# Sparse attention ahead of two feed-forward layers: transposes as two 64-query row tiles, ninth blocks two units at a time, the scale in the minimum pass, input loads spread out

## The chip, the cores and the metric

The kernel runs on one core of a Trainium2 chip. The metric is device time in microseconds (us) of one execution; the median of the runs is compared. TensorE is called PE here, VectorE DVE, ScalarE ACT, GpSimd POOL; SP is the engine whose queue issues most of the DMAs.

## The reference

```python
def _attn_ref(q, k, v, tau):                      # each (4, 8, 576, 64)
    scores = np.matmul(q, k.transpose(0, 1, 3, 2)) / np.sqrt(q.shape[-1])
    thresh = np.max(scores, axis=-1, keepdims=True) - tau
    scores = np.where(scores >= thresh, scores, -1e9)
    attn = np.exp(scores - np.max(scores, axis=-1, keepdims=True))
    attn = attn / (np.sum(attn, axis=-1, keepdims=True) + 1e-09)
    return np.matmul(attn, v)

x = _attn_ref(q, k, v, tau)                       # -> (2304 tokens, 512)
h = x @ w_in;  x = (h * np.tanh(softplus(h))) @ w_out     # 512 -> 2048 -> 512
y = ((x @ w_a) * (x @ w_b)) @ w_out2                      # 512 -> 1536 -> 512
```

The weights of the two feed-forward layers come in as 64-bit floats; the kernel makes 32-bit ones of them.

## The kernel before

Attention runs over 16 pairs of heads (`pairs`), and a pair over five **units** `c` = 0 to 4. Units 0 to 3 are *full*: 128 queries of both heads, so two score rows of 576 keys in each partition. Unit 4 is *half*: the last 64 queries of both heads, stacked on the 128 partitions. There are 80 units, and `attention()` walks them in a software pipeline. In iteration `n` (85 of them) the engines work on different units:

- PE transposes the masked weights of unit n-2 (`turned`), multiplies the transposed weights of unit n-4 with V (`weighted`), and makes the scores of unit n+1 (`scores`);
- DVE takes the minimum of the negated scores of unit n, a head at a time, and copies them out of PSUM in the same pass (`least`), then masks unit n-1 and sums its rows (`mask`); behind the masks of a half unit stands the reciprocal of the sums (`invert`);
- POOL adds tau to the minimum (`bars`, tile `te`), which the mask of the next iteration reads;
- ACT takes the exponential of unit n (`expo`) and copies the transposed blocks from PSUM to SBUF (`pt`, and `pth` for a half unit).

Every engine works in program order. The whole stage is written inside `tc.manual_schedule()`: nothing reorders it.

A full unit's masked weights `pm` are 9 blocks of 128 columns: 576 keys of one head, then 576 of the other. Before, each block is one 128x128 transpose with the identity; blocks 0 to 3, 4 to 7 and 8 fill three buffers of `ps_t`, and the ninth is issued behind the next scores. A half unit has 4 blocks and one of 64 columns. The score matmuls of a full unit work in two row tiles: head 0 on partitions 0 to 63, head 1 on 64 to 127, each into a bank of its own (`sp`, one pair of buffers in all, since a full unit takes both). `weighted` uses two column tiles of 64, and the half unit's scores and the transposes use the whole array.

`scale_q` is an ACT pass over the queries with the factor `nsc` (minus 1/8, or zero for a negative tau), a pair ahead. `convert` walks the 15 weight blocks that are narrowed from 64 to 32 bits inside attention (`narrow`: two passes on ACT, a shift on DVE, an integer addition on POOL, a sign on ACT, a product, then a DMA to DRAM); a block is asked for every fifth unit, so there is one in each pair. Row sums go through `send_inverse` (a transpose, a copy, three small DMAs to `rd`) and come back as a broadcast `inv` (`load_inverse`); `send` multiplies and stores the pair's result to `xd`. From unit 50 on the inputs of the first feed-forward layer are read back (`prepare`) and split in high and low parts between the units, and so is its first weight block.

The feed-forward layers are `pipeline()`: gaps of PE products with ACT and DVE work planned into each. The last results leave through `leave`, from three buffers `ys`.

Of the kernel before, what the change touches and what calls it, by code (L numbers as in the profile page):

```python
# [43 lines left out]
def tile_attn_mish_bilinear(ctx, tc, qd, kd, vd, vd2, tau, w_in, w_out, w_a, w_b, w_out2, out):  # L44
# [427 lines left out]
    def leave(st, ps, c, kind):  # L472

        if kind == "c":
            ys[c] = ys_p.tile([128, 2 * NH], F32, tag="ys", name=f"ys{st.i}_{c}", bufs=3)
        y = ys[c]
        end = st.layer and st.s == NS - 1
        dst = y[:, 0:512] if kind == "c" else y[:, 512:768]
        if end and c % 2:
            V.tensor_copy(dst, ps)  # L480
        else:
            A.activation(dst, ps, AF.Copy)  # L482
        cols = slice(0, 512) if kind == "c" else slice(512, 768)
        if st.layer:
            t0 = 2 * st.s * NH
            (nc.scalar if end and c % 2 else nc.sync).dma_start(
                out=out[c * 128:(c + 1) * 128, t0 + cols.start:t0 + cols.stop], in_=dst
            )
        elif kind != "c":
            nc.scalar.dma_start(out=y1d[st.s][:, c], in_=y)  # L490
# [113 lines left out]
    with late_pools:  # L604
        at = late_pools.enter_context(tc.tile_pool(name="at", bufs=1, side="right"))
        ps_t = late_pools.enter_context(tc.tile_pool(name="ps_t", bufs=3, space=PSUM, side="right"))
# [8 lines left out]
        def load_qk(pi):  # L615
# [4 lines left out]
            qs = qk.tile([128, 640], F32, tag="qs", name=f"qs{pi}", bufs=2)  # L620
# [5 lines left out]
            return dict(q=q, k=k, qs=qs)  # L626

        def scale_q(d, cols):
            A.activation(d["qs"][:, cols], d["q"][:, cols], AF.Copy, scale=nsc)
# [11 lines left out]
        def warm(n):  # L641

            warmed.append(n)
            w = ps_t.tile([128, 4, 128], F32, tag="tp", name=f"warm{len(warmed)}")
# [3 lines left out]
        ph = at.tile([128, 5, 128], F32, name="ph")  # L648
        pth = at.tile([128, 5, 128], F32, name="pth")
# [19 lines left out]
        def scores(u, d):  # L669
# [4 lines left out]
            for half in range(2):  # L674
                keys = slice(half * 288, half * 288 + 288)
                for h, sp in enumerate(u["sp"]):
                    if u["h"] == 2:
                        r, cols = HEADS[h], slice(u["c"] * 128, u["c"] * 128 + 128)
                        PE.matmul(sp[:, half, 0:288], d["qs"][r, cols], d["k"][r, keys], start=True, stop=True)  # L679
                    else:  # L680
                        PE.matmul(sp[:, half, 0:288], d["qs"][:, 512:640], d["k"][:, keys], start=True, stop=True)  # L681

        def least(u, h):

            if h == 0:
# [3 lines left out]
                scalar1=1.0, scalar2=None, op0=ALU.mult, op1=ALU.min, accum_out=u["m"][:, h:h + 1],  # L689
# [29 lines left out]
        def send_inverse(pi):  # L719

            b, p = pairs[pi]
            tp = ps_t.tile([128, 4, 128], F32, tag="tp", name=f"tr{pi}")
            PE.transpose(tp[0:9, 0], pair[pi]["r"], ident)
            rt = at.tile([9, 128], F32, tag="rt", name=f"rt{pi}", bufs=2)
            A.activation(rt, tp[0:9, 0], AF.Copy)
            for h in range(2):
                nc.sync.dma_start(
                    out=rd[p][b][h:h + 1, 0:512].rearrange("o (c n) -> (o c) n", n=128), in_=rt[4 * h:4 * h + 4]
                )
            nc.sync.dma_start(  # L730
                out=rd[p][b][:, 512:576], in_=rt[8:9].rearrange("o (h n) -> o h n", h=2)
            )

        def turned(u, j0, m):

            pm, pt = u["pm"], u["pt"]
            tp = ps_t.tile([128, 4, 128], F32, tag="tp", name=f"tp{u['nm']}_{j0}")
            if u["h"] == 1 and j0 == 4:
                PE.transpose(tp[0:64, 0], pm[:, 4, 0:64], ident)
                return lambda: A.activation(pt[0:64, 4], tp[0:64, 0], AF.Copy)  # L740
# [73 lines left out]
        def attention():  # L814
# [3 lines left out]
            scale_q(data[0], slice(0, 128))  # L818
            warm(6)
            scale_q(data[0], slice(128, 640))  # L820
# [6 lines left out]
            for n in range(len(units) + 5):  # L827
                u, prev, mid = us.get(n), us.get(n - 1), us.pop(n - 2, None)
                old = units[n - 4] if 4 <= n < len(units) + 4 else None
                convert(n, 1)  # L830
                if u:
# [17 lines left out]
                if backs[1:]:  # L849
                    backs[1]()  # L850
# [6 lines left out]
                last = turned(mid, *parts[-1]) if mid else None  # L857
# [4 lines left out]
                if u and c == 3 and pi + 1 < len(pairs):  # L862
                    scale_q(data[pi + 1], slice(0, 640))
                ask(n)
                convert(n, 5)
# [23 lines left out]
                if last:  # L889
                    last()  # L890
                    if mid["c"] == 4:
                        send_inverse(mid["pi"])
# [75 lines left out]
```

## Time and profile before

| | |
|---|---|
| median of 3 runs | 1093.05 us (1092.75 to 1094.0) |
| the profiled execution's own time | 1093.93 us |
| its span, first to last instruction | 1092.1 us |
| PE busy | 1083.9 us, 99% |
| PE weight loads busy | 942.6 us, 86% |
| DVE busy | 813.2 us, 74% |
| ACT busy | 646.8 us, 59% |
| POOL busy | 68.7 us, 6% |
| one pair of heads, 135.70 to 152.54 us | 16.84 us: PE 16.84, DVE 15.11, ACT 15.30, POOL 4.35 |

Attention takes about the first 285 us, the two feed-forward layers the rest. A busy PE is no proof of a PE at its peak, since the ends of matmuls are modelled; starts are recorded, and the distance from one start to the next is what a matmul costs when nothing waits.

### The profile page before, as it was taken

The page shows a single profiled execution, that of the slowest core. Times are in us where ns is not written, and L with a number is a line of the kernel's source. Part 1 is how long each engine was busy: PE and PEld are TensorE (multiplying, and loading weights), DVE is VectorE, ACT ScalarE, POOL GpSimd, SP SyncE. Part 2 cuts the span into 40 slices and gives each one's busy share as a digit, 9 for nine tenths or more (in the row PEclk, how much of TensorE's full clock was granted, in tenths as well). Part 3 has the DMA queues.
Part 4 walks back from the last instruction along what each step waited for, and adds up shares of the span by engine and source line. Part 5 has one row for each costly group of instructions (what it writes and reads, how often), then busy time and mean ns, then how long its engine had stood idle before and what let it go on. Part 6 is the DMA issues. An engine that isn't in the chain of part 4 may idle for free.

```text
span 1092.1 us, 18655 instructions
## 1 busy us (share of the span) xinstructions
PE 1083.9 (99%) x6842; PEld 942.6 (86%) x6842; DVE 813.2 (74%) x1768; ACT 646.8 (59%) x1285; POOL 68.7 (6%) x101
## 2 busy tenths in 40 slices
PE   9999999999999999999999999999999999999998
PEld 7666666666899999999999999999999999999997
DVE  6889889999567787888667897777766657656653
ACT  6999899999656567566565575434343333433321
POOL 2222222222000000000000000000000000000000
PEclk9999999999999999999999999999999999999999
DMA  5456466645669749695498975436314452143401
GB/s 194 132 181 193 144 200 188 200 142 175 197 214 304 256 153 341 252 349 198 164 356 294 318 275 173 156 128 226 129 59 152 159 189 90 49 154 123 170 8 58
DMA packets 77707, 203.14 MB, mean 186 GB/s; under 512 B 6832, under 2 KB 36272, under 8 KB 73776
## 3 DMA queue, kind: packets, MB, share of 16 engines
q1 hardware_dynamic: 73152, 172.29, 47.4%
q10 hardware_dynamic: 4464, 29.66, 6.8%
q8 instruction: 54, 0.88, 0.4%
q14 instruction: 37, 0.30, 0.1%
HBM read 146.01 MB, written 55.91 MB: 185 GB/s over the span
## 4 chain that ended last, share of the span: by engine, by line
PE 97%; ACT 1%; DVE 1%; issue 0%; DMA 0%; ACTq 0%; POOL 0%; POOLq 0%; DVEq 0%
PE acc L462 32%; PE sums_o L761 7%; PE tp L742 7%; PE sp L679 7%; PE sp L681 1%; PE sums_o L765 1%; PE h0i L342 1%; PE warm L646 1%; PE h6i L342 1%; PE h3i L342 1%; PE h7i L342 1%; PE h5i L342 1%; PE h4i L342 1%; PE h2i L342 1%; PE h1i L342 1%; PE h15i L361 1%
## 5 line engine op out<-in xcount | busy, mean ns | idle before, releaser
L462 PE MATMUL acc<-g,woo 128*128 128x256 f32 (+1 forms) x1152 | 225.3, 338 | 0.0
L462 PEld LDWEIGHTS acc<-g,woo 128*128 128x128 f32 x1152 | 181.2, 188 | 16.7
L462 PE MATMUL acc<-g,wop 128*128 128x512 f32 (+1 forms) x864 | 170.7, 338 | 0.0
L462 PEld LDWEIGHTS acc<-g,wop 128*128 128x128 f32 x864 | 137.4, 188 | 13.4 <-DVE g L391 0.8
L687 DVE TENSOR_SCALAR_CACHE_REDUCE s<-sp 128x576 f32<-128x576 f32 x144 | 103.8, 755 | 28.5 <-PE sp L679 24.8
L699 ACT ACTIVATE ex<-s,m 128x576 f32<-128x576 f32 x144 | 109.9, 776 | 5.5 <-DVE s L687 5.5
L743 ACT ACTIVATE pt<-tp 128x512 f32<-128x512 f32 (+1 forms) x192 | 92.4, 494 | 15.3 <-PE tp L742 12.2
L706 DVE SCALAR_TENSOR_TENSOR pm<-s,te,ex 128x576 f32<-128x576 f32 x128 | 99.5, 815 | 0.0
L742 PEld LDWEIGHTS tp<-ident,pm 128*128 128x128 f32 x576 | 64.0, 141 | 23.8 <-ACT ex L699 11.1
L761 PE MATMUL sums_o<-pt,v 128*64 128x256 f32 x640 | 83.2, 389 | 0.3 <-ACT u L771 0.3
L385 DVE TENSOR_TENSOR g<-hs,g 128x384 fp32r<-128x384 f32 x96 | 51.8, 554 | 40.1 <-ACT g L384 32.3
L742 PE MATMUL tp<-ident,pm 128*128 128x128 f32 x576 | 80.2, 278 | 0.6 <-ACT pt L743 0.2
L679 PE MATMUL sp<-k,qs 64*128 64x288 f32 x512 | 80.4, 429 | 0.0
L679 PEld LDWEIGHTS sp<-k,qs 64*128 64x128 f32 x512 | 45.0, 186 | 29.9 <-issue 15.6
L761 PEld LDWEIGHTS sums_o<-pt,v 128*64 128x64 f32 x640 | 40.2, 136 | 25.1 <-issue 5.9
L694 POOL TENSOR_TENSOR te<-m,bar 128x2 f32<-128x2 f32 (+1 forms) x80 | 48.8, 610 | 175.5 <-DVE s L687 175.3
L482 ACT ACTIVATE ys<-acc 128x512 f32<-128x512 f32 (+1 forms) x44 | 21.3, 488 | 30.9 <-PE acc L462 25.4
L390 ACT ACTIVATE g<-s 128x384 fp32r<-128x384 f32 x18 | 9.5, 525 | 39.9 <-DVE s L441 39.6
L390 ACT ACTIVATE g<-c22b 128x384 fp32r<-128x384 f32 x18 | 9.5, 527 | 37.3 <-DVE c22b L441 37.3
L178 DVE TENSOR_TENSOR woo<-wfo,woo 128x512 fp32r<-128x512 f32 x46 | 30.5, 684 | 0.0
L177 ACT ACTIVATE woo<-wfo 128x512 fp32r<-128x512 f32 x46 | 26.7, 627 | 3.0 <-PE acc L462 2.6
L416 DVE TENSOR_TENSOR c22a<-u3a,p5a 128x384 f32<-128x384 f32 x18 | 10.0, 556 | 21.1 <-ACT p5a L414 21.0
(638 smaller groups left out, 2148.1 us busy)
## 6 DMA issues: line engine op xcount, KB each, us to landing
wia<-wpa SPq DMA_DIRECT2D x10, 1792.0 KB
wpi<-wii ACTq DMA_DIRECT2D x7, 1792.0 KB
wii<-wpi SPq DMA_DIRECT2D x7, 1792.0 KB
wfo<-wfo SPq DMA_DIRECT2D x23, 512.0 KB
wpa<-wia ACTq DMA_DIRECT2D x6, 1792.0 KB
v<-vd SPq DMA_DIRECT2D x16, 576.0 KB
rawi<-w_in SPq DMA_DIRECT2D x16, 512.0 KB
rawo<-w_out SPq DMA_DIRECT2D x16, 512.0 KB
```

Source lines behind the costliest of these rows:

```text
L178: lambda: V.tensor_tensor(out=dst()[1], in0=src(), in1=f32(dst()[0]), op=ALU.subtract),
L342: PE.matmul(st.bank, w[:, a, 2 * i + j, c * 128:(c + 1) * 128], x[:, b, c], start=j == c == m == 0, stop=j == c == 1 and m == 2,)
L385: at_gap(gap + 1, lambda: V.tensor_tensor(out=gl, in0=hs, in1=f32(gh), op=ALU.subtract))
L462: PE.matmul(ps, w[:, a, f, c * 128:(c + 1) * 128], st.g[f][:, b, cols], start=st.first and f == 0 and m == 0 and (kind == "c" or c % 2 == ...
L679: PE.matmul(sp[:, half, 0:288], d["qs"][r, cols], d["k"][r, keys], start=True, stop=True)
L687: V.tensor_scalar(out=u["s"][:, h].rearrange("p (a c) -> p a c", a=2), in0=u["sp"][h][:, :, 0:288], scalar1=1.0, scalar2=None, op0=ALU.mul ...
L694: G.tensor_tensor(out=u["te"][:, :n], in0=u["m"][:, :n], in1=bar2[:, :n], op=ALU.add)
L699: A.activation(u["e"][:, h], u["s"][:, h], AF.Exp, bias=u["m"][:, h:h + 1], scale=-1.0)
L706: V.scalar_tensor_tensor(out=u["pm"].rearrange("p a c -> p (a c)")[:, h * S:(h + 1) * S], in0=u["s"][:, h], scalar=u["te"][:, h:h + 1], in ...
L742: PE.transpose(tp[:, i], pm[:, j0 + i], ident)
L743: return lambda: A.activation(pt[:, j0:j0 + m], tp[:, :m], AF.Copy)
L761: PE.matmul(po[r], v[0][:, j + 4 * h, r], pair[pi][c & ~1][:, :, j + 4 * h], start=j == 0, stop=j == 4)
```

## The change

1. **Transposes.** Blocks 0 to 7 of a full unit become two transposes each, of 64 queries (partitions 0 to 63, then 64 to 127) by 128 keys, into two buffers of their own (`tp0`, `tp1`). A half unit has five blocks of this kind; the missing 64 columns of its last one are set to zero once. Each buffer leaves in one ACT copy.
2. **Ninth blocks.** Those of units 0 and 1, and of 2 and 3, are transposed together as whole 128x128 blocks behind the transposes of the later unit, into a third buffer (`tc`), and leave in one copy. The transpose of the inverse sums goes into the same buffer.
3. **Scale.** `scale_q` is gone; `nsc` is the scalar operand of the minimum pass, a value per partition where there was the constant 1.0.
4. **Narrowing.** The product moves from DVE to POOL, and from five units behind the due time to three, where it stands ahead of that unit's `te`.
5. **Order.** `load_inverse` and `send` come two iterations later. The four input loads come at units 49, 54, 59 and 64, their splits from 52 to 70, the first weight block from 66 to 78.
6. **End.** The last wide result of the program gets a buffer of its own.

```diff
@@ narrow @@
-        V.tensor_tensor(out=o, in0=a.bitcast(F32), in1=o, op=ALU.mult)
+        (G if early else V).tensor_tensor(out=o, in0=a.bitcast(F32), in1=o, op=ALU.mult)
@@ leave @@
+            if end and c == 3:
+                ys[c] = raw.tile([128, 2, NH], F32, tag="b00", name=f"ys{st.i}_{c}", bufs=1).rearrange("p i n -> p (i n)")
+            else:
+                ys[c] = ys_p.tile([128, 2 * NH], F32, tag="ys", name=f"ys{st.i}_{c}", bufs=3)
@@ load_qk, scores, least @@
-        def scale_q(d, cols):
-            A.activation(d["qs"][:, cols], d["q"][:, cols], AF.Copy, scale=nsc)
...
-                        PE.matmul(sp[:, half, 0:288], d["qs"][r, cols], d["k"][r, keys], start=True, stop=True)
+                        PE.matmul(sp[:, half, 0:288], d["q"][r, cols], d["k"][r, keys], start=True, stop=True)
...
-                scalar1=1.0, scalar2=None, op0=ALU.mult, op1=ALU.min, accum_out=u["m"][:, h:h + 1],
+                scalar1=nsc, scalar2=None, op0=ALU.mult, op1=ALU.min, accum_out=u["m"][:, h:h + 1],
@@ turned @@
-        def turned(u, j0, m):
...
-            for i in range(m):
-                PE.transpose(tp[:, i], pm[:, j0 + i], ident)
-            return lambda: A.activation(pt[:, j0:j0 + m], tp[:, :m], AF.Copy)
+        def turned(u):
+
+            n = 8 if u["h"] == 2 else 5
+            tiles = [ps_t.tile([128, 8, 64], F32, tag=f"tp{h}", name=f"tp{u['nm']}_{h}") for h in range(2)]
+            for j in range(n):
+                for h, r in enumerate(HEADS):
+                    PE.transpose(tiles[h][:, j], u["pm"][r, j], ident[r, r])
+            moves = [lambda h=h: A.activation(u["pt"][:, 0:n, HEADS[h]], tiles[h][:, 0:n], AF.Copy) for h in range(2)]
+            if u["c"] in (1, 3):
+                t = u["turn"] = ps_t.tile([128, 4, 128], F32, tag="tc", name=f"tc{u['nm']}")
+                both = u["pair"][u["c"] - 1]
+                for i, pm in enumerate((u["pair"]["pm"], u["pm"])):
+                    PE.transpose(t[:, i], pm[:, 8], ident)
+                moves.append(lambda: A.activation(both[:, :, 8], t[:, 0:2], AF.Copy))
+            u["pair"]["pm"] = u["pm"]
+            return moves
@@ attention @@
                 convert(n, 1)
+                convert(n, 3)
...
-                    parts = ((0, 4), (4, 4), (8, 1)) if mid["h"] == 2 else ((0, 4), (4, 1))
-                    backs = [turned(mid, j, m) for j, m in parts[:-1]]
+                    backs = turned(mid)
...
-                last = turned(mid, *parts[-1]) if mid else None
...
-                convert(n, 5)
...
-                if 3 <= n < len(units) + 3 and units[n - 3][1] == 4:
-                    load_inverse(units[n - 3][0])
-                if 8 <= n < len(units) and units[n - 8][1] == 4:
-                    send(units[n - 8][0])
+                if n in range(9, len(units), 5) or n == len(units) + 2:
+                    load_inverse((n - 9) // 5 + (n > len(units)))
+                if 10 <= n < len(units) and units[n - 10][1] == 4:
+                    send(units[n - 10][0])
...
-                if n == 50:
+                if n == 48:
                     loads, rest = prepare(0, 0)
-                    for load in loads:
-                        load()
-                    plan(55, [(2 * k, item) for k, item in rest])
+                    plan(0, zip((49, 59, 64, 54), loads))
+                    plan(0, zip((52, 55, 57, 60, 62, 65, 67, 70), (item for _, item in rest)))
+                if n == 66:
                     load, rest = first_weights(0)
                     load()
-                    plan(56, [(2 * k, item) for k, item in enumerate(rest)])
+                    plan(0, zip((71, 72, 74, 73, 78), rest))
```

On PE, this is what stood in the second pair between the scores of its unit 0 and of its unit 1, where unit 3 of the first pair is transposed (`tp_3`); a matmul of 32-bit floats in such a list is two instructions in the trace, a transpose is one:

```order
L742 MATMUL tp_2_8_388<-ident,pm_2_270 128x128
L742 MATMUL tp_3_0_410<-ident,pm_3_306 128x128 x4
L742 MATMUL tp_3_4_415<-ident,pm_3_306 128x128 x4
L761 MATMUL sums_o<-pt_0_227,v_220 64x256 x4
L679 MATMUL sp_1_0_431<-k_216,qs_217 128x288
L679 MATMUL sp_1_1_432<-k_216,qs_217 128x288
```

In the changed kernel, at the same place (the last four of sixteen narrow transposes are shown):

```order
L742 MATMUL tp_3_0_424<-ident,pm_3_311 128x64
L742 MATMUL tp_3_1_425<-ident,pm_3_311 128x64
L742 MATMUL tp_3_0_424<-ident,pm_3_311 128x64
L742 MATMUL tp_3_1_425<-ident,pm_3_311 128x64
L748 MATMUL tc_3_442<-ident,pm_2_267 128x128
L748 MATMUL tc_3_442<-ident,pm_3_311 128x128
L769 MATMUL sums_o<-pt_0_224,v_217 64x256 x4
L679 MATMUL sp_1_0_457<-k_214,qr_213 128x288
L679 MATMUL sp_1_1_458<-k_214,qr_213 128x288
```

The ninth block of unit 2 has moved behind the narrow transposes of unit 3, beside the ninth of unit 3, and the scores of a full unit are now followed by narrow transposes, which work in the same two row tiles.

On POOL, one pair's instructions stood like this (`ai` and `ao` are the narrowing's additions):

```order
L112 TENSOR_TENSOR ai_614<-ai_614,unit 128x512
L694 TENSOR_TENSOR te_0_600<-m_0_599,bar_82 128x2
L694 TENSOR_TENSOR te_1_651<-m_1_650,bar_82 128x2
L694 TENSOR_TENSOR te_2_687<-m_2_686,bar_82 128x2
L694 TENSOR_TENSOR te_3_735<-m_3_734,bar_82 128x2
```

And now:

```order
L112 TENSOR_TENSOR ai_658<-ai_658,unit 128x512
L694 TENSOR_TENSOR te_0_648<-m_0_647,bar_82 128x2
L694 TENSOR_TENSOR te_1_707<-m_1_706,bar_82 128x2
L123 TENSOR_TENSOR fi_659<-ai_658,fi_659 128x512
L694 TENSOR_TENSOR te_2_748<-m_2_747,bar_82 128x2
L694 TENSOR_TENSOR te_3_796<-m_3_795,bar_82 128x2
```

The narrowing's product (L123) now stands between `te` of unit 1 and `te` of unit 2; on DVE it stood between the minimum of the half unit and the masks of unit 3.

## Rows read from the trace of the kernel before

**Rows 1.** The page: the granted PE clock in 40 slices, in tenths of full speed.

```profile
PEclk9999999999999999999999999999999999999999
```

**Rows 2.** Stretches: length; PE, weight loads, DVE, ACT, POOL busy; clock; DMA.

```profile
135.70:152.54 16.84, 16.84 (x142) 11.21 (x140) 15.11 (x42) 15.30 (x32) 4.35 (x7) 1.00 0.58 171
...
285.00:1087.00 802.00, 801.50 (x4574) 752.55 (x4572) 566.69 (x1103) 396.43 (x783) 0.00 (x0) 1.00 0.54 190
```

**Rows 3.** PE in order of time within one pair: start us, length us, instruction, count.

```profile
136.86 1.15 PE L742 MATMUL tp<-ident,pm 128*128 128x128 f32 x9
137.94 1.51 PE L761 MATMUL sums_o<-pt,v 128*64 128x256 f32 x12
139.38 1.24 PE L679 MATMUL sp<-k,qs 64*128 64x288 f32 x8
140.56 1.20 PE L742 MATMUL tp<-ident,pm 128*128 128x128 f32 x9
141.69 1.08 PE L761 MATMUL sums_o<-pt,v 128*64 128x256 f32 x8
...
143.87 0.33 PE L742 MATMUL tp<-ident,pm 128*128 128x128 f32 x1
...
144.57 1.51 PE L761 MATMUL sums_o<-pt,v 128*64 128x256 f32 x12
...
151.75 0.95 PE L765 MATMUL sums_o<-pth,v 128*64 128x64 f32 x20
152.63 1.24 PE L681 MATMUL sp<-k,qs 128*128 128x288 f32 x4
153.70 1.15 PE L742 MATMUL tp<-ident,pm 128*128 128x128 f32 x9
```

**Rows 4.** PE's weight loads in order of time: one pair of row tiles.

```profile
150.04 0.19 PEld L679 LDWEIGHTS sp<-k,qs 64*128 64x128 f32 x2
```

**Rows 5.** DVE in order of time, one iteration of full units, and its wait.

```profile
161.50 0.75 DVE L687 TENSOR_SCALAR_CACHE_REDUCE s<-sp 128x576 f32<-128x576 f32 x1
...
162.18 0.81 DVE L706 SCALAR_TENSOR_TENSOR pm<-s,te,ex 128x576 f32<-128x576 f32 x1
...
164.13 0.76 DVE L687 TENSOR_SCALAR_CACHE_REDUCE s<-sp 128x576 f32<-128x576 f32 x1 [0.39 <-PE sp L679]
```

**Rows 6.** DVE in order of time: behind the half unit's scores; a product of two tensors.

```profile
153.90 0.76 DVE L687 TENSOR_SCALAR_CACHE_REDUCE s<-sp 128x576 f32<-128x576 f32 x1 [0.19 <-PE sp L681]
...
154.59 0.69 DVE L123 TENSOR_TENSOR fo<-ao,fo 128x512 f32<-128x512 f32 x1
...
166.97 0.75 DVE L783 TENSOR_TENSOR u<-u,inv 128x576 f32<-128x576 f32 x1
```

**Rows 7.** POOL in order of time: at the start, and in the pair of rows 5.

```profile
9.56 0.20 POOL L694 TENSOR_TENSOR te<-m,bar 128x2 f32<-128x2 f32 x1 [8.26 <-DVE s L687]
...
157.23 1.28 POOL L112 TENSOR_TENSOR ai<-ai,unit 128x512 int32<-128x512 int32 x1 [1.91 <-ACT unit L107]
...
162.40 0.64 POOL L694 TENSOR_TENSOR te<-m,bar 128x2 f32<-128x2 f32 x1 [2.68 <-DVE s L687]
```

**Rows 8.** ACT's groups in attention: busy us, mean ns, idle before.

```profile
L743 ACT ACTIVATE pt<-tp 128x128 f32<-128x128 f32 x64 | 18.0, 282 | 7.0 <-PE tp L742 5.8
L629 ACT ACTIVATE qs<-qr,nsc 128x640 f32<-128x640 f32 x15 | 12.6, 838 | 0.0
```

**Rows 9.** DVE and PE in order of time: transposes that waited for a mask.

```profile
204.05 0.81 DVE L706 SCALAR_TENSOR_TENSOR pm<-s,te,ex 128x576 f32<-128x576 f32 x1
...
205.02 1.15 PE L742 MATMUL tp<-ident,pm 128*128 128x128 f32 x6 [0.16 <-DVE pm L706]
```

**Rows 10.** PE in order of time: unit 0's scores, second and last pair.

```profile
21.51 0.51 PE L679 MATMUL sp<-k,qs 64*128 64x288 f32 x2
...
259.23 0.51 PE L679 MATMUL sp<-k,qs 64*128 64x288 f32 x2
```

**Rows 11.** The end, in order of time: DVE's copy of the last wide result.

```profile
1087.36 0.69 DVE L480 COPY ys<-acc 128x512 f32<-128x512 f32 x1 [1.43 <-DMA out_t<-ys]
```

More of the change, by code (lines that the diff above doesn't have):

```diff
@@ L472, in leave @@
     def leave(st, ps, c, kind):
+        end = st.layer and st.s == NS - 1
         if kind == "c":
-            ys[c] = ys_p.tile([128, 2 * NH], F32, tag="ys", name=f"ys{st.i}_{c}", bufs=3)
+            if end and c == 3:
+                ys[c] = raw.tile([128, 2, NH], F32, tag="b00", name=f"ys{st.i}_{c}", bufs=1).rearrange("p i n -> p (i n)")
+            else:
+                ys[c] = ys_p.tile([128, 2 * NH], F32, tag="ys", name=f"ys{st.i}_{c}", bufs=3)
         y = ys[c]
-        end = st.layer and st.s == NS - 1
         dst = y[:, 0:512] if kind == "c" else y[:, 512:768]
@@ L605, in tile_attn_mish_bilinear @@
         at = late_pools.enter_context(tc.tile_pool(name="at", bufs=1, side="right"))
-        ps_t = late_pools.enter_context(tc.tile_pool(name="ps_t", bufs=3, space=PSUM, side="right"))
+        ps_t = late_pools.enter_context(tc.tile_pool(name="ps_t", bufs=1, space=PSUM, side="right"))
         ps_o = late_pools.enter_context(tc.tile_pool(name="ps_o", bufs=1, space=PSUM, side="right"))
@@ L619, in load_qk @@
             k = qk.tile([128, S], F32, tag="k", name=f"k{pi}", bufs=3)
-            qs = qk.tile([128, 640], F32, tag="qs", name=f"qs{pi}", bufs=2)
             first = 128 if pi == 0 else 640
@@ L625, in load_qk @@
                 nc.sync.dma_start(out=q[:, first:], in_=qd[b, p][:, first:])
-            return dict(q=q, k=k, qs=qs)
-        def scale_q(d, cols):
-            A.activation(d["qs"][:, cols], d["q"][:, cols], AF.Copy, scale=nsc)
+            return dict(q=q, k=k)
         def load_v(pi):
@@ L643, in warm @@
             warmed.append(n)
-            w = ps_t.tile([128, 4, 128], F32, tag="tp", name=f"warm{len(warmed)}")
+            w = ps_t.tile([128, 4, 128], F32, tag=f"tp{len(warmed) % 2}", name=f"warm{len(warmed)}")
             for _ in range(n):
@@ L648, in tile_attn_mish_bilinear @@
         ph = at.tile([128, 5, 128], F32, name="ph")
+        G.memset(ph[:, 4, 64:128], 0.0)
         pth = at.tile([128, 5, 128], F32, name="pth")
@@ L678, in scores @@
                         r, cols = HEADS[h], slice(u["c"] * 128, u["c"] * 128 + 128)
-                        PE.matmul(sp[:, half, 0:288], d["qs"][r, cols], d["k"][r, keys], start=True, stop=True)
+                        PE.matmul(sp[:, half, 0:288], d["q"][r, cols], d["k"][r, keys], start=True, stop=True)
                     else:
-                        PE.matmul(sp[:, half, 0:288], d["qs"][:, 512:640], d["k"][:, keys], start=True, stop=True)
+                        PE.matmul(sp[:, half, 0:288], d["q"][:, 512:640], d["k"][:, keys], start=True, stop=True)
         def least(u, h):
@@ L717, in invert, with send_inverse @@
             V.reciprocal(r, sm)
-        def send_inverse(pi):
+        def send_inverse(pi, tp):
             b, p = pairs[pi]
[L722 to L732, printed above, removed]
@@ L734, in turned @@
-        def turned(u, j0, m):
[L736 to L740, printed above, removed]
-            for i in range(m):
-                PE.transpose(tp[:, i], pm[:, j0 + i], ident)
-            return lambda: A.activation(pt[:, j0:j0 + m], tp[:, :m], AF.Copy)
+            tp = tp[0:9, 3]
@@ new lines, in send_inverse, with leave @@
+            PE.transpose(tp, pair[pi]["r"], ident)
+            def leave():
+                rt = at.tile([9, 128], F32, tag="rt", name=f"rt{pi}", bufs=2)
+                A.activation(rt, tp, AF.Copy)
+                for h in range(2):
+                    nc.sync.dma_start(
+                        out=rd[p][b][h:h + 1, 0:512].rearrange("o (c n) -> (o c) n", n=128), in_=rt[4 * h:4 * h + 4]
+                    )
+                nc.sync.dma_start(out=rd[p][b][:, 512:576], in_=rt[8:9].rearrange("o (h n) -> o h n", h=2))
@@ new lines, in send_inverse @@
+            return leave
+        def turned(u):
[13 more added lines that the diff above has]
+            return moves
@@ L817, in attention @@
             data, vs = {0: load_qk(0)}, {}
-            scale_q(data[0], slice(0, 128))
             warm(6)
-            scale_q(data[0], slice(128, 640))
             data[1] = load_qk(1)
@@ L843, in attention @@
                 if mid:
-                    parts = ((0, 4), (4, 4), (8, 1)) if mid["h"] == 2 else ((0, 4), (4, 1))
-                    backs = [turned(mid, j, m) for j, m in parts[:-1]]
+                    backs = turned(mid)
+                    done_pair = mid["pi"] - (mid["c"] < 4)
+                    if mid["c"] == 1 and mid["pi"]:
+                        backs.append(send_inverse(done_pair, mid["turn"]))
+                    if mid["c"] == 4 and mid["pi"] == len(pairs) - 1:
+                        backs.append(send_inverse(done_pair, ps_t.tile([128, 4, 128], F32, tag="tc", name="tcend")))
                     backs[0]()
@@ L848, in attention @@
                     expo(u, 0)
-                if backs[1:]:
-                    backs[1]()
+                for move in backs[1:]:
+                    move()
                 back = weighted(*old, vs[old[0]]) if old else None
@@ L861, in attention @@
                     back()
-                if u and c == 3 and pi + 1 < len(pairs):
-                    scale_q(data[pi + 1], slice(0, 640))
                 ask(n)
-                convert(n, 5)
                 convert(n, 0)
```

4 lines of the change are left out of this document (removed).

## Prediction

> **What bounds the kernel now.** I read the page first, then stretches, then PE's starts, and last DVE, POOL and ACT in one pair of heads. The granted clock is full everywhere (2.4 GHz) [rows 1], so no time here comes from the clock. In the stretches see that PE has no idle time in a pair, nor in the feed-forward layers [rows 2]: whatever attention loses, the program loses, and 800 us behind it stay as they are. A pair takes 16.84 us, and DVE with 15.11 and ACT with 15.30 are close behind [rows 2]. So two things have to be worked out: what PE's work shrinks to, and who holds it up then.
>
> PE's starts give the price list [rows 3]. Nine transposes behind the half unit's scores take 1.08 (136.86 to 137.94); behind two-row-tile scores 1.13 (140.56 to 141.69); five take 0.70 (143.87 to 144.57). Four more cost 1.13 - 0.70 = 0.43: **0.109 us for a whole block**. The 0.05 between 1.13 and 1.08 is the first weight load, open where the array's tiling has just changed and hidden where it has not. Eight score matmuls in row tiles take 1.18, four whole ones of the same width 1.07, and only the first are followed by a change of tiling: **a change costs about 0.1** (the unrounded starts give 0.09), and two row tiles take the time of one.
>
> **The narrow transposes.** No row of this trace has one. Nearest are two rows. Twenty matmuls of 64 columns, in ten column-tile pairs, take 0.88 from 151.75 to 152.63 [rows 3]; less two changes (0.18) and two open loads (0.1) that is 0.06 a pair. And two weight loads of 64x128 in row tiles lie within 0.19, the length that one has alone [rows 4]: they run side by side. So I take **0.058 for a block** of two narrow transposes. From below it can't be much less than half of 0.109; from above, one after the other, it is again 0.11.
>
> PE per pair, with 4 x 8 + 5 = 37 such blocks: 37 x (0.109 - 0.058) = 1.89 off. Scores and narrow transposes share a tiling, so four changes with their open load go: 4 x 0.147 = 0.59 off. Ninth blocks cost what they did, but twice the array has to change for them: 2 x 0.147 = 0.29 on. Behind the half unit's scores, which use the whole array, there is one change that was not there: 0.15 on. Sum: 16.84 - 2.04 = **14.8 us of PE per pair**.
>
> **ACT** loses `scale_q` (0.84) and four copies of 0.28 for two wider ones [rows 8]: some 14 of 15.30. It is not the next bound, unless copies into two 64-wide halves cost over 0.1 more each. The Trainium skill, TensorEngine Tiling (Array Packing), section PSUM Bottleneck, warns of this: packing speeds TensorE up, and emptying PSUM may become the limit. By that rule the time would be ACT's; by the rows ACT stays below the sum that follows.
>
> **DVE** loses the product: 0.69 [rows 6], less the 0.07 by which a DVE instruction overhangs the next one's start (0.75 long, the next 0.68 later [rows 5]), so 15.11 - 0.6 = 14.5. The minimum gets its factor from a tensor. Bounds: nothing, or what the mask, which has such a scalar, takes more than a plain product of the same size, 0.81 - 0.75 = 0.06 [rows 5, 6]. Between, I take 0.03 in nine passes: 0.3. The product on POOL I price like the addition there, 1.28 [rows 7]. Ahead of unit 2's `te` it has to fit beside two minimum passes (2 x 0.68 by the starts in rows 5). `te` took 0.20 with DVE idle and 0.64 beginning under a mask, where it ended only with that mask [rows 5, 7]: POOL and a mask exclude each other. I put 0.1 per pair for a mask that waits for POOL, between 0 and 0.6. DVE: 14.9.
>
> **The chain between the two.** Neither 14.8 nor 14.9 is the period, because PE and DVE wait for each other. A mask's end (unit n-1) releases its transposes; behind them on PE stand the sums and the scores of unit n+2; these release the minimum, and behind that on DVE stands the mask of n+1. One such round takes two iterations, and with five units in a pair it passes every PE leg and every DVE leg once in two pairs. PE legs: 14.8, plus five handovers. DVE began 0.20 behind the start of PE's next group (153.70 to 153.90) [rows 3, 6], and transposes began 0.16 after the mask's end (204.86 to 205.02) [rows 9]; 5 x 0.36 = 1.8. Off goes what PE does under the second mask: four blocks of each full unit need only the first head, 4 x 4 x 0.058 = 0.93. That makes 15.7. DVE legs: 14.9. Per pair (15.7 + 14.9) / 2 = **15.3 us**. Before, with 16.84 on PE, this chain had slack; DVE's wait of 0.39 for scores shows it [rows 5].
>
> **The sum.** From the second pair's first scores to the last pair's are 14 pairs and 237.72 us [rows 10], 14 x 16.84 = 235.76 and 1.96 that PE lost while the layer's inputs were split. I keep that loss at 2.8: the same splits, spread out, but into a chain without slack. 14 x 15.3 + 2.8 = 217.0: 20.7 saved. The first pair, which waits on start-up and still holds its warm-up matmuls: 0.5. The last pair and its drain, up to 2.04 by PE's work, but with masks to wait for: 1.6. The end: DVE's last wide copy waited 1.43 for a DMA that frees a buffer [rows 11]; with its own buffer it waits for PE alone, and ACT's issue and copies behind it move up too: 1.1. Together 23.9. The profiled execution took 1093.93, 0.9 above the median of 1093.05; off the median, **1069 us**.
>
> The later `load_inverse` and `send` I cost at nothing: they have iterations of 3 us to spare, and SP, which now waits for POOL's product ahead of the small stores to `rd`, has nothing urgent behind it there (V's loads come two iterations later). If that cover went, a pair's inverse would come late and DVE would wait in `send`.
>
> **Rivals.**
> - *PE stays the bound* (14.8): DVE's handovers hide, and the minimum's scalar is free. 14 x 14.8 + 2.0 = 209.2, 28.5 saved; with 0.5 + 2.0 + 1.1 it is 32.1: 1061. For it: PE had no idle time at all in a pair. Against it: DVE's 14.5 is too near.
> - *DVE or ACT becomes the bound* (15.8): 0.06 in each minimum, 0.6 of masks held by POOL, 0.07 for a block. PE legs 15.9, DVE legs 15.7. 14 x 15.8 + 2.8 = 224: 13.7 saved, with 0.5 + 1.1 + 1.1 some 16.4: 1076.7. For it: the mask's extra 0.06 and `te`'s 0.64.
> - *The row tiles do not pair in transposes* (0.11 a block): PE 14.8 + 1.9 = 16.7. 14 x 0.14 = 2.0, with 0.5 and 1.1 some 3.6: 1089.5; at 0.116 some 1.4 saved, 1091.6. Against it: rows 3 and 4, though they are no transposes.
> - *POOL's product holds DVE up*: slower. If it misses the minimum passes and takes the port when a mask is due, that mask waits up to 1.28, `te` of unit 2 behind it runs late, and its mask waits the same again: 2.6 per pair on the chain, 17.9, so 14 x 1.06 = 14.8 more, less 3 elsewhere: 1105. It decides from 1.7 us of such waits in each pair. The Trainium skill, SBUF — State Buffer, section Who interferes with whom, states it as a lock: a DVE instruction with two SBUF inputs and a GpSimd one that reads SBUF block each other for a whole instruction. `te`'s 0.20 against 0.64 agrees. Against the rival: the addition, as long, fits under minimum passes today, and the mask after it begins on time.
>
> **How the numbers follow.** Chances: the forecast (periods of 15.0 to 15.5, 1065 to 1072) 0.50; PE stays the bound 0.15; DVE or ACT 0.24; unpaired row tiles 0.08; POOL 0.03. The range of 1061 to 1077 leaves out the last two and the edges of the second and third. Faster by over 0.2% (2.2 us, about what a measurement here can tell): the first three and most of the fourth, 0.95; within it 0.02; slower 0.03.
>
> **What would show it.** Right: starts of narrow transposes 0.058 apart in pairs, some 0.5 for a full unit's sixteen and no gap from the scores; a pair from one unit 0's scores to the next in 15.3; short waits of transposes for `pm` and of scores for `s` on PE, which the steady pairs lack now; DVE's idle time before the minimum nearly gone; no `scale_q`; the feed-forward layers as long as before. Wrong: narrow transposes 0.11 apart or with a gap at each change of head; a minimum of 0.82 instead of 0.76; masks that begin where POOL's L123 ends; ACT without idle time. The prediction fails most easily in the 15.3, which rests on legs that I added up from single rows.

## The result and the profile after

| | before | after |
|---|---|---|
| median of 5 runs each, same chip | 1093.42 us (1092.75 to 1094.0) | 1084.55 us (1083.83 to 1085.03) |
| ratio, 95% interval | | 0.9917 [0.9905, 0.9928] |
| span of the profiled execution | 1092.1 us | 1082.8 us |

The kernel is faster by 8.9 us. The forecast was 1069, with 1061 as the low and 1077 as the high end: the direction was right, and the saving 15 us too large.

The page of the changed kernel, against [rows 1, 2, 5]: its span, the engines, the clock, and the minimum pass (busy us, mean ns, then idle time ahead and what ended it).

```profile
span 1082.8 us, 19717 instructions
PE 1067.1 (99%) x7434; PEld 938.3 (87%) x7434; DVE 813.2 (75%) x1753; ACT 628.5 (58%) x1236; POOL 91.8 (8%) x117
PEclk9999999999999999999999999999999999999999
L687 DVE TENSOR_SCALAR_CACHE_REDUCE s<-sp,nsc 128x576 f32<-128x576 f32 x144 | 112.5, 815 | 19.6 <-PE sp L679 14.1
```

The minimum pass on the page of the kernel before:

```profile
L687 DVE TENSOR_SCALAR_CACHE_REDUCE s<-sp 128x576 f32<-128x576 f32 x144 | 103.8, 755 | 28.5 <-PE sp L679 24.8
```

PE is as busy in share as before and works 17 us less. The minimum is 0.815 long; it was 0.755, so its scalar costs 0.06, the upper bound.

PE in one pair after, the answer to [rows 3], by starts:

```profile
84.75 1.24 PE L679 MATMUL sp<-k,qr 64*128 64x288 f32 x8
85.82 0.66 PE L742 MATMUL tp<-ident,pm 64*128 64x64 f32 x16
86.42 0.44 PE L748 MATMUL tc<-ident,pm 128*128 128x128 f32 x2
...
88.88 0.48 PE L742 MATMUL tp<-ident,ph 64*128 64x64 f32 x10
89.64 1.52 PE L769 MATMUL sums_o<-pt,v 128*64 128x256 f32 x12 [0.28 <-ACT u L779]
...
92.16 0.66 PE L742 MATMUL tp<-ident,pm 64*128 64x64 f32 x16
92.75 1.08 PE L769 MATMUL sums_o<-pt,v 128*64 128x256 f32 x8
93.77 1.45 PE L679 MATMUL sp<-k,qr 64*128 64x288 f32 x8
94.84 1.08 PE L742 MATMUL tp<-ident,pm 64*128 64x64 f32 x16
95.85 0.44 PE L748 MATMUL tc<-ident,pm 128*128 128x128 f32 x2
...
100.47 0.51 PE L679 MATMUL sp<-k,qr 64*128 64x288 f32 x2
```

Sixteen narrow transposes take 0.59 (92.16 to 92.75), the change of tiling behind them included; the first and the last of them start 0.438 apart, seven steps of 0.062. Scores followed by them take 1.07 where they took 1.17. The pair is 15.72 long (84.75 to 100.47). The sums are the products of the transposed weights with V. Two places in the pair are too long: ten transposes of a half unit take 0.76 (88.88 to 89.64), since the sums behind them wait for ACT's copy `u`; and the sixteen of unit 1 take 1.01 (94.84 to 95.85), 0.42 more than those of unit 0. Free of waits the ten take 0.40 (102.80 to 103.20 in a kernel further below). So the two waits cost 0.36 + 0.42 = 0.78, and **PE's own work is 15.72 - 0.78 = 14.94 per pair**. The longer one is a wait for a mask: the ninth of the sixteen, the first that needs the second head, starts at 95.46, 0.06 behind the end of the second mask (95.40).

Where the input of the first feed-forward layer is read back and split, pairs are longer. ACT from 163 to 252 us, the split's row (busy, mean ns, idle ahead):

```profile
L290 ACT ACTIVATE x<-b 128x768 fp32r<-128x768 f32 x4 | 3.4, 844 | 4.7 <-DMA b<-xd 4.7
```

The chain of waits there (start, us, what):

```profile
162.83 1.57 SPq L635
...
164.57 0.53 SPq L785
...
165.19 0.42 SPq L792
...
165.66 0.42 SPq L274
...
166.14 9.73 DMA b<-xd
...
175.95 0.07 ACT x L290
```

SP issues V's loads (L635), the inverse (L785), the store of a result (L792) and then the layer's inputs (L274), which land 9.7 us later. Their split stands three units behind the load, some 9.4 us, and ACT waits. PE at that place:

```profile
175.83 1.24 PE L681 MATMUL sp<-k,qr 128*128 128x288 f32 x4
177.33 0.27 PE L742 MATMUL tp<-ident,pm 64*128 64x64 f32 x1 [0.26 <-ACT pt L743]
178.48 0.71 PE L742 MATMUL tp<-ident,pm 64*128 64x64 f32 x15 [0.88 <-ACT pt L743]
179.65 2.00 PE L769 MATMUL sums_o<-pt,v 128*64 128x256 f32 x12 [0.47 <-ACT u L778]
181.58 2.29 PE L679 MATMUL sp<-k,qr 64*128 64x288 f32 x8
183.66 0.79 PE L742 MATMUL tp<-ident,pm 64*128 64x64 f32 x16
```

And the stretches behind it (the granted clock is the third number from the end):

```profile
180.00:181.00 1.00, 1.00 (x10) 0.60 (x8) 1.00 (x4) 1.00 (x3) 0.00 (x0) 0.77 0.01 1
181.00:182.00 1.00, 1.00 (x6) 0.42 (x4) 0.36 (x2) 1.00 (x3) 0.04 (x1) 0.50 0.75 253
182.00:183.00 1.00, 1.00 (x6) 0.72 (x6) 0.00 (x0) 0.39 (x1) 1.00 (x1) 0.50 0.94 334
183.00:184.00 1.00, 1.00 (x12) 0.61 (x12) 0.09 (x1) 0.00 (x0) 0.22 (x1) 0.52 0.97 317
184.00:185.00 1.00, 1.00 (x18) 0.71 (x17) 1.00 (x3) 0.51 (x2) 0.00 (x0) 1.00 1.31 344
```

After the waits PE's clock stands at 1.2 GHz (0.50) for some three microseconds, and eight scores take 2.08 (181.58 to 183.66) instead of 1.07. With the twelve sums ahead of them (1.93 instead of 1.45) and the transposes behind (0.72 instead of 0.59) that is some 1.6 us. The page's row of 40 slices doesn't show it. The Trainium skill, TensorE: Matmul & The Clock Gate, section HAM oscillation — how this bites in real kernels, says that PE's waits for transfers bring its clock down. This trace agrees in direction, with 0.50 behind 1.6 us of recorded waits; here PE waited for ACT, and ACT for the transfer.

### The profile page after: what moved, and what is told of

Read it like the earlier page. It is cut to its first block, busy times and chain, and to the rows that moved or that the text cites. A ratio compares the mean times of both kernels' runs of the same rounds, so it can differ in the third digit from the quotient of the medians.

```text
span 1082.8 us, 19717 instructions
## 1 busy us (share of the span) xinstructions
PE 1067.1 (99%) x7434; PEld 938.3 (87%) x7434; DVE 813.2 (75%) x1753; ACT 628.5 (58%) x1236; POOL 91.8 (8%) x117
## 4 chain that ended last, share of the span: by engine, by line
PE 86%; ACT 5%; DMA 4%; DVE 3%; issue 2%; SPq 1%; ACTq 0%; POOL 0%; DVEq 0%; POOLq 0%
PE acc L462 32%; PE sums_o L769 4%; PE sp L679 4%; PE tp L742 3%; ACT ex L699 2%; DMA b<-xd 2%; ACT pt L743 1%; PE sp L681 1%; DVE pm L706 1%; DVE s L687 1%; DMA inv<-rd 1%; PE sums_o L773 1%; PE h2i L342 1%; PE h5i L342 1%; PE h7i L342 1%
## 5 line engine op out<-in xcount | busy, mean ns | idle before, releaser
L687 DVE TENSOR_SCALAR_CACHE_REDUCE s<-sp,nsc 128x576 f32<-128x576 f32 x144 | 112.5, 815 | 19.6 <-PE sp L679 14.1
L743 ACT ACTIVATE pt<-tp 128x512 f32<-128x512 f32 x128 | 75.2, 588 | 22.3 <-PE tp L742 21.0
L679 PE MATMUL sp<-k,qr 64*128 64x288 f32 x512 | 86.5, 434 | 0.0
L679 PEld LDWEIGHTS sp<-k,qr 64*128 64x128 f32 x512 | 51.2, 188 | 29.7 <-issue 15.4
L694 POOL TENSOR_TENSOR te<-m,bar 128x2 f32<-128x2 f32 (+1 forms) x80 | 52.8, 660 | 129.7 <-DVE s L687 102.5
L742 PEld LDWEIGHTS tp<-ident,pm 64*128 64x128 f32 x1024 | 45.8, 139 | 19.0 <-ACT pt L743 6.1
L742 PE MATMUL tp<-ident,pm 64*128 64x64 f32 x1024 | 53.1, 227 | 4.0 <-ACT pt L743 3.4
L290 ACT ACTIVATE x<-b 128x768 fp32r<-128x768 f32 x24 | 20.2, 843 | 11.1 <-DMA b<-xd 4.7
```

The costliest lines, as they stand in the source:

```text
L679: PE.matmul(sp[:, half, 0:288], d["q"][r, cols], d["k"][r, keys], start=True, stop=True)
L687: V.tensor_scalar(out=u["s"][:, h].rearrange("p (a c) -> p a c", a=2), in0=u["sp"][h][:, :, 0:288], scalar1=nsc, scalar2=None, op0=ALU.mul ...
L694: G.tensor_tensor(out=u["te"][:, :n], in0=u["m"][:, :n], in1=bar2[:, :n], op=ALU.add)
L742: PE.transpose(tiles[h][:, j], u["pm"][r, j], ident[r, r])
L743: moves = [lambda h=h: A.activation(u["pt"][:, 0:n, HEADS[h]], tiles[h][:, 0:n], AF.Copy) for h in range(2)]
```

## The experiments

The steady pair below is the mean of seven, from the start of the third pair's first scores to the tenth's (37.69 to 147.65 after: 15.71). The split stage is from the eleventh's to the sixteenth's (163.36 to 250.38 after: 87.02; five steady pairs would be 78.5, so it loses 8.5). Both are read from the profiled execution, the medians are of 4 to 8 runs; before took 1093.25, 1093.57 or 1093.81 beside them.

| kernel | median, us | ratio to before | steady pair | split stage |
|---|---|---|---|---|
| changed kernel | 1084.55 | 0.9917 [0.9905, 0.9928] | 15.71 | 87.02 |
| e1_splits_later | 1078.7 | 0.9864 [0.9848, 0.988] | 15.71 | 80.8 |
| e1_loads_first | 1078.69 | 0.9865 [0.9851, 0.988] | 15.71 | 80.8 |
| e2_constant | 1081.35 | 0.9886 [0.9871, 0.9901] | 15.48 | 85.9 |
| e3_u_first | 1082.12 | 0.9897 [0.9882, 0.9911] | 15.60 | 86.0 |
| c1_three | 1072.84 | 0.9806 [0.9793, 0.982] | 15.35 | 79.6 |
| c2_no_product | 1072.51 | 0.9803 [0.9787, 0.982] | 15.39 | 79.5 |
| c3_two | 1077.41 | 0.985 [0.9835, 0.9865] | 15.60 | 80.8 |
| c4_pool_scale | 1080.31 | 0.9877 [0.9863, 0.989] | 15.69 | 83.5 |
| e4_dve_product | 1090.77 | 0.9975 [0.9964, 0.9985] | 16.27 | 88.1 |
| e5_transposes_alone | 1087.35 | 0.9937 [0.9924, 0.9949] | 15.90 | 89.3 |

**The split stage, two ways.** One edit gives the loads more time before they are needed, the other issues them one unit earlier, ahead of V's loads.

```diff
-  plan(0, zip((52, 55, 57, 60, 62, 65, 67, 70), (item for _, item in rest)))
+  plan(0, zip((57, 60, 62, 65, 67, 70, 72, 75), (item for _, item in rest)))   # e1_splits_later
-  plan(0, zip((49, 59, 64, 54), loads))
+  plan(0, zip((48, 58, 63, 53), loads))                                        # e1_loads_first
```

> The changed kernel, with the four splits of the first layer's input five iterations later (57 to 75 instead of 52 to 70; the loads stay at 49, 54, 59, 64). Theory 1: between units 50 and 78 ACT sits in front of a split whose input is still on its way (one took 9.7 us from issue to landing, three iterations are 9.4 us); with eight iterations it has long landed. Expected: no wait of ACT for b<-xd, the five pairs from the eleventh pair's first scores to the last pair's fall from 87.0 us to about 81 to 82, the whole from 1084.5 to 1079. Rival: the splits' own work on ACT and DVE overloads a chain without slack; then those pairs stay at 86 to 87 and the whole within 1 us.

> The changed kernel, with the four input loads one iteration earlier (48, 53, 58, 63), where they are issued ahead of V's loads (0.9 MB) and not behind them; the splits stay where they are. Theory 1 (the splits wait for loads that queue behind others): landing falls from 9.7 to about 4 us, no wait of ACT for b<-xd, the whole at about 1079. Rival (work of the splits): within 1 us of 1084.5. If the DMA engines are simply full there, whatever the order, landing stays at 7 us or more, and half of the waits go: 1082.

Both take 5.9 us off. ACT's row in e1_loads_first, same stretch:

```profile
L290 ACT ACTIVATE x<-b 128x768 fp32r<-128x768 f32 x4 | 3.4, 841 | 0.0
```

The wait of 4.7 is gone, the granted clock of the stage is 1.00 again, and the stage loses 80.8 - 78.5 = 2.3. So it was the time from issue to use, with nothing taken from the splits themselves, and the rival falls. Whether the loads land sooner in e1_loads_first, as expected, the run doesn't show, since nothing waits for them any more; the place ahead of V's loads and the unit gained are not told apart.

**The minimum's scalar.** The constant minus 1/8 in place of the tensor leaves out the zero factor for a negative tau.

```diff
-  scalar1=nsc, scalar2=None, op0=ALU.mult, op1=ALU.min, ...
+  scalar1=-SCALE, scalar2=None, op0=ALU.mult, op1=ALU.min, ...
```

> The changed kernel, with the factor of the minimum pass as the constant -1/8 in place of the scalar per partition (what is left out: a negative tau, for which that scalar is zero). Theory 2: the scalar costs DVE 0.06 us in each of nine passes of a pair, and half of these 0.54 us reach the period by the chain of masks, transposes, scores and minimum. Expected: the pass back at 0.755 us, the steady pair from 15.72 to 15.45, the whole 4 us less (1080.5). Rival: the period is set by PE and by its waits for ACT's copies; then the pass is as short, but the pair stays at 15.65 or more and the whole within 1 us.

The pass is 0.75 again and the pair 0.23 shorter: less than half of the 9 x 0.06 = 0.54 that DVE saves. Both waits of the pair shrink, the ten transposes of the half unit to 0.65 (87.07 to 87.72) and the sixteen of unit 1 to 0.89 (92.92 to 93.81), together by 0.11 + 0.12. The first pair, from its first scores to the next pair's, gets shorter by nearly all of it, from 14.97 to 14.49.

**The copy that the sums wait for.** ACT copies `u` ahead of the second exponential, not behind it.

```diff
-                if u and u["h"] == 2:
-                    expo(u, 1)
...
+                if u and u["h"] == 2:
+                    expo(u, 1)
```

> The changed kernel, with ACT's copy of the finished sums ahead of the second exponential instead of behind it. Theory 3: the next sums wait 0.3 us in each pair for that copy, and the wait is on the path. Expected: no wait of sums for u, the steady pair from 15.72 to 15.45, the whole 4 us less (1080.5). Rival: the copy itself then waits for PE's sums and holds up the exponential behind it, so the mask comes later: pair unchanged or up to 0.3 longer, the whole between 1084.5 and 1089.

PE's sums from 53 to 160 us in the changed kernel, with their idle time:

```profile
L769 PE MATMUL sums_o<-pt,v 128*64 128x256 f32 x272 | 35.5, 389 | 2.0 <-ACT u L779 2.0
```

and in e3_u_first:

```profile
L769 PE MATMUL sums_o<-pt,v 128*64 128x256 f32 x272 | 35.5, 389 | 0.0
```

The wait is gone, some 0.3 a pair, and the pair is only 0.11 shorter: most of the rest came back at the transposes of unit 0, which now took 0.75 (91.48 to 92.23) instead of 0.59, and of unit 1, 1.05 (94.35 to 95.40) instead of 1.01.

**All three, and what bounds then.** c1_three joins e1_loads_first, e2_constant and e3_u_first.

> The changed kernel with the input loads at 48, 53, 58, 63, the constant -1/8 in the minimum pass (a negative tau is left out) and ACT's copy of the sums ahead of the second exponential. If the three losses are separate, their gains add: steady pair 15.72 - 0.23 - 0.12 = 15.37, the stretch of the splits without waits for loads, the whole near 1073.5. If PE's own work is the floor (14.8 forecast; with the measured 0.062 a block 14.95), the pair can't fall below 14.95. Rival: the waits share one cause, then the pair stays at 15.48 and the whole at 1075.

The three add up. PE and DVE in it at the place of the one long wait that is left:

```profile
104.59 1.24 PE L679 MATMUL sp<-k,qr 64*128 64x288 f32 x8
...
105.67 0.72 PE L742 MATMUL tp<-ident,pm 64*128 64x64 f32 x16
...
106.00 0.76 DVE L687 TENSOR_SCALAR_CACHE_REDUCE s<-sp 128x576 f32<-128x576 f32 x1
...
106.68 0.75 DVE L687 TENSOR_SCALAR_CACHE_REDUCE s<-sp 128x576 f32<-128x576 f32 x1
...
107.36 0.81 DVE L706 SCALAR_TENSOR_TENSOR pm<-s,te,ex 128x576 f32<-128x576 f32 x1
...
108.10 0.81 DVE L706 SCALAR_TENSOR_TENSOR pm<-s,te,ex 128x576 f32<-128x576 f32 x1
...
108.41 1.03 PE L742 MATMUL tp<-ident,pm 64*128 64x64 f32 x16
...
109.37 0.44 PE L748 MATMUL tc<-ident,pm 128*128 128x128 f32 x2
```

In this unit PE has eight sums and not twelve, so 2.74 from transposes to transposes (105.67 to 108.41). DVE's four passes take 2.91 (106.00 to 108.91) and start 0.33 later: the second mask is late, the ninth transpose starts 0.06 behind its end (108.97), and the sixteen take 0.96 instead of 0.59. The next kernel takes DVE work away elsewhere in the pair: the product of `u` with the inverse sums, so that the results of attention are not divided.

```diff
-            V.tensor_tensor(out=d["u"], in0=d["u"], in1=d["inv"], op=ALU.mult)
```

> c1_three without the product of u with the inverse sums (L791, 0.67 us of DVE in each pair by its starts), so the results of attention are not divided by their sums. Theory (a chain that passes every PE leg and every DVE leg once in two pairs): a pair gets shorter by half of it, 0.34, from 15.35 to 15.0, and the program by some 5.0 us, to 1068. Rival 1, DVE alone sets the period: by 0.67, to 14.7. Rival 2, PE alone sets it: nothing, 15.35 and 1072.8.

The pair stays (15.39 against 15.35: six of the seven pairs take some 15.35, and the one of the rows below 15.59, by a further wait for a mask in unit 2). PE in it at the half unit and at the late mask:

```profile
102.80 0.47 PE L742 MATMUL tp<-ident,ph 64*128 64x64 f32 x10
103.20 1.52 PE L769 MATMUL sums_o<-pt,v 128*64 128x256 f32 x12
...
108.46 1.03 PE L742 MATMUL tp<-ident,pm 64*128 64x64 f32 x16
109.42 0.44 PE L748 MATMUL tc<-ident,pm 128*128 128x128 f32 x2
```

The minimum pass from 53 to 160 us in c1_three, then in c2_no_product:

```profile
L687 DVE TENSOR_SCALAR_CACHE_REDUCE s<-sp 128x576 f32<-128x576 f32 x63 | 45.5, 755 | 5.5 <-PE sp L679 2.8
L687 DVE TENSOR_SCALAR_CACHE_REDUCE s<-sp 128x576 f32<-128x576 f32 x63 | 45.5, 756 | 9.7 <-PE sp L679 6.7 <-DVE pm L706 0.5
```

The late mask stands unchanged (108.46 to 109.42), and the time saved on DVE turns up as its wait for scores, 6.7 us and not 2.8. So the chain as the prediction had it, in which every DVE leg counts half, does not hold here. Rival 2 gave the right number; the cause is PE's 14.94 with one wait of 0.37.

**Two of the three, for any tau.**

> The changed kernel with two of the edits of c1_three, for any tau: the input loads at units 48, 53, 58 and 63, ahead of V's loads, and the copy of u ahead of the second exponential; the minimum keeps its scalar per partition. If the two are independent: 1084.55 less 5.9 (first edit alone) less 2.4 (second alone) = 1076.3 us, a steady pair of 15.60 and pairs 10 to 15 in some 80.3. If the minimum's scalar, which stays, takes the second edit's gain back once the loads no longer cover it: a pair of 15.7 and 1078.6.

The steady pair is 15.60 and the time, 1077.41, is 1 us above the sum of the two edits. It is the fastest of these kernels that leaves nothing out.

**The scale on POOL.** c4_pool_scale has the two edits of c3_two, a pass of POOL over the queries a pair ahead (two on the first pair), and the constant 1.0 in the minimum.

```diff
+        def scale_q(d, cols):
+            G.tensor_scalar(out=d["qs"][:, cols], in0=d["q"][:, cols], scalar1=nsc, scalar2=None, op0=ALU.mult)
...
-                scalar1=nsc, scalar2=None, op0=ALU.mult, op1=ALU.min, ...
+                scalar1=1.0, scalar2=None, op0=ALU.mult, op1=ALU.min, ...
```

> The changed kernel with the loads at 48, 53, 58, 63, the copy of the sums first, and the queries scaled by POOL once a pair (in unit 2's iteration, behind its te) so that the minimum pass gets its constant 1.0 back; this holds for any tau. If POOL has the room (28% busy in a pair), it is as fast as the version with the constant, near 1073.5, pair 15.37. Rival: the 640 columns hold POOL and its port for about 1 us while masks run; masks or te wait and the pair is back at 15.7 or longer, the whole at 1079 or more.

POOL and DVE in it:

```profile
95.15 1.89 POOL L632 TENSOR_SCALAR qs<-qr,nsc 128x640 f32<-128x640 f32 x1 [2.09 <-DMA qr<-qd]
...
95.24 1.31 DVE L710 SCALAR_TENSOR_TENSOR pm<-s,te,ex 128x576 f32<-128x576 f32 x1
```

POOL's pass takes 1.89 and began just ahead of a mask, which took 1.31 instead of 0.81. The Trainium skill, SBUF — State Buffer, section Who interferes with whom, states that a DVE instruction with two SBUF inputs contends with a GpSimd one that reads SBUF, by an exclusive lock, and that whoever issues first holds the shared ports for the whole instruction. The row agrees that the second to come, the mask, is held up, but it ended at 96.55, half a microsecond ahead of POOL's end in the record. In all six places of this trace where a mask began 0.09 to 0.42 behind the start of such a pass of 1.89, it ended 1.40 or 1.41 behind that start. Less the mask's own 0.81 that is a hold of 0.59, and not of the whole pass. The rival was right: the pair is 0.09 longer than in c3_two, where the scalar stays in the minimum, and the whole took 1080.31.

**The product back on DVE.**

```diff
-        (G if early else V).tensor_tensor(out=o, in0=a.bitcast(F32), in1=o, op=ALU.mult)
+        V.tensor_tensor(out=o, in0=a.bitcast(F32), in1=o, op=ALU.mult)
```

> The changed kernel with the narrowing's product back on DVE (at its new place, three units behind). Theory 2 (half of DVE's work reaches the period by the chain): 0.62 us more on DVE lengthens the pair by about 0.27 to 0.3, 15.72 to 16.0, the whole by 4 us to 1088.5. Rival (PE and ACT alone set the period): within 1 us. Rival of the prediction (POOL's product holds masks up): faster than 1084.5.

The whole is 6.2 us slower, and each pair 0.56 longer, most of DVE's 0.6. Here the DVE leg counts nearly whole: it stands directly ahead of the minimum of unit 2 and the masks of unit 1, which PE waits for anyway. PE's scores there take 1.57 (96.66 to 98.23) and not 1.07, their second bank held until 97.40, 0.06 behind that minimum's end. L791 counted nothing. So it depends on where in the pair the pass stands; the two were measured in different kernels, and what the difference between these adds is not shown.

**The transposes alone.** Before with parts 1 and 2 of the change, and `load_inverse` and `send` two units later; the scale on ACT, the product on DVE, the loads in one burst at unit 50 and the end are as before.

> The kernel before with the transposes and ninth blocks of the changed one alone: the queries scaled by ACT, the constant in the minimum, the product on DVE five units behind, all input loads at unit 50 and their splits from 55, no buffer of its own at the end (the inverse's later load belongs to the moved transpose and stays). Theory: DVE has 0.54 less in the minimum and 0.62 more in the product, so the pair is as in the changed kernel, 15.7 to 15.8, or up to 0.2 longer by ACT's 0.84; no wait for input loads, but splits and first weights together: 3 to 4 us lost there. The whole near 1081 to 1083: faster than the changed kernel, and the transposes alone carry its gain. Rival: without the other parts the transposes gain little, 1088 or more.

It saves 6.2 us, where the whole change saves 8.9, and less than expected. The steady pair is 15.90, and the split stage loses 89.3 - 79.5 = 9.8. PE there:

```profile
195.64 1.51 PE L773 MATMUL sums_o<-pt,v 128*64 128x256 f32 x12
200.30 1.63 PE L683 MATMUL sp<-k,qs 64*128 64x288 f32 x8 [3.14 <-ACT qs L632]
```

The scores wait 3.14 for `scale_q`, which waits 3.85 for the next pair's queries, which stand on SP behind the burst and land 10.73 after their issue. From 200 to 205 us the granted clock is 0.60 and from 205 to 210 it is 0.72. This kernel's times go with the clock: a mean granted clock of 1.0 took 1084.44, 0.998 took 1085.42, 0.997 took 1087.35, and 0.996 took 1087.67 and 1088.35. So spreading the loads had a reason: with the shorter pairs the burst is in the way of the queries. The change exchanged that wait for its own.

## Why the prediction was wrong in size

By the span the saving is 9.3, the forecast 23.9: 14.6 are missing.

| term | forecast | measured | missing |
|---|---|---|---|
| fourteen pairs, split stage included | 217.0 | 228.29 (22.09 to 250.38) | 11.3 |
| start and first pair | 0.5 off | 0.58 more | 1.1 |
| last pair and drain | 1.6 off | 0.1 off | 1.5 |
| end | 1.1 off | 0.8 off | 0.3 |
| feed-forward layers | 0 | 0.4 more | 0.4 |

Two steps failed, by about as much each: the loss kept for the split stage, and the way in which the chain adds waits up.

**The split stage, kept at 2.8.** It measured 8.5, 5.7 too much. I took the loss of before for a price of the splits. The landing of a load was not among the costs of the step that was moved, though its DMA now stood behind V's 0.9 MB on SP and its use three units behind. This is shown by two edits, each of which brings the loss to 2.3; so the price of the splits themselves was nearly right. In the changed kernel some 1.6 us of the loss is PE at 1.2 GHz (180 to 184 us); in the profiled executions of e2_constant and e3_u_first the stage's clock was 1.00, ACT waited more for the loads (6.3 and 7.5 us), and the stage still lost 8.5 (85.9 - 5 x 15.48) and 8.0 (86.0 - 5 x 15.60). So such waits make this loss with the clock or without it. The clock seems to come on top: e2_constant took 1079.87 at a mean clock of 1.0, and 1081.31 to 1081.43 in its three other runs, at 0.997 and 0.998.

**The chain, 15.3: too short by 0.41, 5.7 us over fourteen pairs.** PE's legs were nearly right: 14.94 against 14.8, a narrow block 0.062 against 0.058, no change of tiling between scores and transposes. With the measured legs put in (PE 14.94 + 1.8 - 16 x 0.062, DVE 15.04 in the pair shown) the chain gives 15.4, so sizes make some 0.1 of the miss and the mechanism 0.3. Wrong was how waits were added. An average over a round of two pairs lets a DVE pass count half wherever it stands; measured, L791 counts nothing, L123 nearly all, the minimum's scalar 0.23 of 0.54. A pair is PE's work and the waits at single places: 0.42 for a second mask where PE has eight sums and DVE four passes, and 0.36 for the copy of `u`, an ACT leg that the chain did not hold at all. With that copy moved and the scalar gone, in c1_three, a pair takes 15.35, and 15.35 less its one wait of 0.37 leaves 14.98 for PE. The scalar was mis-sized too: 0.06, twice what I took. That 15.3 and c1_three's 15.35 nearly agree is by chance.

**Emptying PSUM.** ACT is not full (14.27 of the pair's 15.72 us), but one of its copies out of PSUM did hold PE, by its place behind an exponential (e3_u_first) and not by its length. The rule that the prediction weighed, in the Trainium skill, TensorEngine Tiling (Array Packing), section PSUM Bottleneck, had that much of a point.

**The first pair.** I counted half a microsecond off. The minimum's scalar lengthens it instead, 14.97 against 14.49 with the constant. The first scores began at 7.12 against 6.76 before; across the kernels profiled here it was 6.50 to 7.57, so 0.4 of it says nothing of the change.

**The last pair and drain.** I counted 1.6 of PE's 2.04; measured 0.1, and 1.0 in c1_three (24.73 against 25.75). There PE waits for DVE and ACT with nothing else to do. Which of the waits took what in it stays open.

**Right.** Faster; the narrow transposes pair; at the end the last wide copy no longer waits for the DMA that frees a buffer [rows 11]; the product on POOL is no hindrance. It takes 1.28, DVE's masks keep their 0.815 on average, and with the product back on DVE the kernel is 6.2 us slower. The forecast's price of 0.1 for masks held by POOL and the rival of 1105 both found nothing to show for them, though c4_pool_scale shows that such holding is real, there for 0.59 us of a pass of 1.89. Of the signs, a minimum of 0.82 stood among those of being wrong, and came; DVE's idle time before it did not nearly go, but fell from 28.5 to 19.6 us. The rival with DVE or ACT as the bound had nearly the right period (15.8) by another way. In the rival of unpaired row tiles one sum is off, with no effect on the rest: at 0.116 a block PE comes to 16.95 and 0.1 us is saved, not 1.4.

## What to carry to other kernels

When a pair gets shorter, add waits place by place, not as an average: list for every unit what each engine does there, and look for the unit in which the second engine has more work than the first. When a load is moved, count its way from issue to landing in units of the new, shorter period, behind all that its queue holds then. And look where a removed wait goes: of 0.3 taken from one place only 0.11 left the pair, the rest came back at the next. The three edits alone gave 5.9, 3.2 and 2.4 us, and together 11.7, beyond the 8.9 of the change itself.

## Not expected of the hardware

- A scalar per partition instead of a constant costs a DVE pass of 576 columns 0.06 us (0.815 against 0.755), although the pass reads PSUM and is otherwise the same.
- PE's clock fell to 1.2 GHz in the middle of the program behind three recorded waits of PE of 0.26, 0.88 and 0.47 us, while the row of 40 slices shows full clock.
- A POOL pass of 1.89 us held masks that began behind its start only until 0.59 us from that start (c4_pool_scale).
